# A state-space scan and a long convolution on one core: scanning pairs of time steps, and a written order for the instructions

## The chip, the cores and the metric

The kernel runs on one NeuronCore of one Trainium2 chip. The metric is the device time in microseconds of one execution. A core has TensorE (PE, matrix products into PSUM), VectorE (DVE), ScalarE (ACT), GpSimd (POOL) and SyncE (SP). Here SP, POOL and ACT also issue the DMA transfers, which sixteen DMA engines carry. Each engine works through its own instructions in the order in which the program gave them, and semaphores make one engine wait for another.

## The reference, cut to what matters

Two independent layers with L = 2048 times and D = 640 channels; their results stand side by side in the output.

```
# A: diagonal complex state space, 640 states
Lam_bar = exp(dt * Lam);  B_bar = ((Lam_bar - 1) / Lam)[:, None] * Bmat
h[t] = Lam_bar * h[t-1] + B_bar @ x[t]
a[t] = 2 * real(C @ h[t]) + Dskip * x[t]
# B: a shift of 4 taps on k, then a causal convolution over all 2048 times per channel
k_shift[t] = sum_j k[t-j] * shift_k[:, j]          # j = 0..3
kv = k_shift * v
y  = irfft(rfft(kv, 2L) * rfft(ssm_k, 2L))[:L]  + kv * ssm_D
b  = q * y
```

## The kernel before

**Layer A** goes by 4 chunks of 512 times (c) and 5 blocks of 128 states (j); n = 5c + j. `load_x` turns a chunk of x into `xT` on SP's queue. `pe_z` (L423) makes z = B x, 10 products of 512 columns for real and imaginary part; ACT moves z from PSUM to SBUF (L677). DVE rotates z by the phase of the state (`rotate`, L434 to L436, three steps of 1024 elements), which makes the recurrence real; it then scans with the real decay (`dve_scan`, L443, two scans of 512), and rotates back (`dve_out`). At the end of a chunk the last state is kept and turned by the phase of 512 steps (`dve_carry`). `pe_proj` (L466) multiplies h with C and (L472) adds D x through a diagonal matrix: for each of the 16 rows of 128 times 5 pieces, one per state block, each as soon as its h is there. ACT evicts (L476, `yo`), POOL stores (L480). Before that, C is multiplied by the complex factor of each state on PE (`pe_cs`, L349), with diagonal matrices that DVE builds (`dve_dg`, L335), and evicted by ACT (L353). B is turned on PE (L395).

**Layer B** goes by 5 groups G of 128 channels. `load_T` turns k and v on SP. The four taps are products of diagonal 128x128 matrices with shifted columns of kT (`pe_tap`, L509, 8 of 512 columns for each half of the times); DVE multiplies with v (L514). The convolution is a long transform in two steps: kv goes to DRAM and back so that rows of 128 times lie in the partitions (`store_kv`, `load_kv`); ssm_k is loaded in the same shape (`load_h`). The first step `pe_s1` (L525) has 16 products of 256 columns, the second `pe_s2` (L538 to L541) 64 of 128 columns, for kv and for ssm_k each; ACT evicts all of them (L529, L544). DVE multiplies the spectra (`dve_y`, L551 to L556). `pe_inv` (L565 to L568, 64 products) goes back, ACT evicts into `zz` (L572), SP turns zz into `Zt` (`turn_z`, L576), `pe_fin` (L586, 32 products) finishes, DVE multiplies with q (L591, `ob`), POOL stores (L596) and loads q (L580).

**The order.** `make_plan` lists the pieces of work with their engine, an assumed cost, what they depend on, and which piece takes or gives back one of the four double PSUM banks. `Plan.order` simulates the engines with those costs and a table of priorities (`PRIO`), and emits the pieces in the order that comes out. A name like `s2h3_1` is: second transform step of ssm_k for group 3, quarter 1; `s1k`, `s2k` the same for kv; `he`/`ke` endings are evictions; `tap`, `kv`, `kvo`, `kvs`, `y`, `inv`, `zs`, `zt`, `qi`, `fin`, `ob` follow the steps above; `p`, `yo`, `yd` are projection, eviction, store. SP's queue carries in order: x, k, v, C, h and the turns of zz; one entry that waits holds those behind it:

```
dma(f"zt{G}", "SP", 4.8, 3.7, [zs{G}_0..3] + [fin{G-1}_0, fin{G-1}_1], K.turn_z)
A(f"fin{G}_{hf}", "PE", 16 * P128, [f"zt{G}", "dRM"], ...)
A(f"ob{G}_{hf}", "DVE", PTT, [f"fin{G}_{hf}", f"qi{G}"], ...)
```

Of the kernel before, what the change touches and what calls it, by code (L numbers as in the profile page):

```python
# [22 lines left out]
NCH = L // CW  # L23
# [3 lines left out]
NH = 8  # L27
NPS = 4


class Plan:
# [5 lines left out]
    def add(self, name, eng, cost, deps=(), fn=None, lat=0.0, take=None, give=None, group=None):  # L37
        assert name not in self.items, name
        if eng == "PE":
            lat = max(lat, 0.2)  # L40
        self.items[name] = (eng, cost, [d for d in deps if d], fn, lat, take, give, group)

    def order(self, prio, hop=0.15):
        it = self.items
        succ = {n: [] for n in it}
        for n, x in it.items():
            for d in x[2]:
                succ[d.lstrip("~")].append(n)
        tail = {}
        todo = {n: len(succ[n]) for n in it}  # L50
        stack = [n for n in it if not todo[n]]
        while stack:
            n = stack.pop()
            x = it[n]
            tail[n] = x[1] + x[4] + max([tail[s] for s in succ[n]], default=0.0)
            for d in x[2]:
                d = d.lstrip("~")
                todo[d] -= 1
                if not todo[d]:
                    stack.append(d)  # L60
        assert len(tail) == len(it), [n for n in it if n not in tail][:5]
        rank = {n: -(tail[n] + prio.get(it[n][7], 0.0)) for n in it}
        need = {n: len(it[n][2]) for n in it}
        ready = {}
        for n in it:
            ready.setdefault(it[n][0], [])
            if not need[n]:
                ready[it[n][0]].append(n)
        free = dict.fromkeys(ready, 0.0)
        slots = [0.0] * NPS  # L70
        held, slot_of, done, start, seq = {}, {}, {}, {}, []
        while len(seq) < len(it):
            best = None
            for e, names in ready.items():
                c = []
                for n in names:
                    t = free[e]
                    for d in it[n][2]:
                        if d[0] == "~":
                            t = max(t, start[d[1:]] + it[d[1:]][1])  # L80
                        else:
                            t = max(t, done[d] + (hop if it[d][0] != e else 0.0))
                    if it[n][5] and it[n][5] not in held:
                        s = min(slots)
                        if s > 1e8:
                            continue
                        t = max(t, s)
                    c.append((t, rank[n], n))
                if c:
                    t0 = min(c)[0]  # L90
                    p, t, n = min((p, t, n) for t, p, n in c if t <= t0 + 0.05)
                    if best is None or (t, p) < best[:2]:
                        best = (t, p, n, e)
            t, _, n, e = best
            x = it[n]
            ready[e].remove(n)
            start[n], free[e], done[n] = t, t + x[1], t + x[1] + x[4]
            if x[5]:
                if x[5] not in held:
                    i = max((s, -i) for i, s in enumerate(slots) if s <= t + 1e-9)[1]  # L100
                    held[x[5]] = -i
                    slots[-i] = 1e9
                slot_of[n] = held[x[5]]
            if x[6]:
                slot_of[n] = held[x[6]]
                slots[held[x[6]]] = done[n] + hop
            seq.append((t, len(seq), n))
            for s in succ[n]:
                need[s] -= 1
                if not need[s]:  # L110
                    ready[it[s][0]].append(s)
        self.start, self.done = start, done
        return [n for _, _, n in sorted(seq)], slot_of


class Kernel:


    def __init__(self, ctx, tc, out, ins):
# [12 lines left out]
        t("ident", [128, 128])  # L132
        t("pidx", [128, 1], i32)
        t("c26", [128, 1], i32)
        for n in ("lre", "lim", "ldt", "dsk"):
            t(n + "_raw", [128, NT])
        for n in ("lre", "lim", "ldt", "dtf", "theta", "rho", "rr", "fr", "kf", "sin1", "aph1", "cos1", "nr", "ni", "den",
                  "t0", "rden", "g2re", "g2im", "ra"):
            t(n, [128, NT], f32)
# [4 lines left out]
        t("gb", [128, NT, 6])  # L144
        t("rots", [128, NT, 2], f32)
        t("rotc", [128, NT, 2], f32)
        for n in ("ca", "cb"):
            t(n, [128, NT, 2], f32)
        for i in range(2):
            t(f"last{i}", [128, NT, 2], f32)  # L150
            t(f"carry{i}", [128, NT, 2], f32)
        for n, k in (("r_hi", 1), ("r_lo", 1), ("bsh", 1), ("m_kk", 1), ("m_lo", 1), ("m_k1h", 1), ("m_ri", 1), ("m_k4", 2),
                     ("ccol", 8), ("r_ph", 32), ("r_q16", 32), ("m_ph", 32)):
            t(n, [128, k], i32)
        t("r_mask", [128, 8])
        t("m_mask", [128, 8])
        t("r_aph", [128, 32], f32)
        t("m_aph", [128, 32], f32)
        t("r_cv", [128, 32])
        t("m_cv", [128, 32], f32)  # L160
        t("sk_b", [128, NG, 4])
        t("dcol_b", [128, 16 * NG])
        t("lo", [128, CW], i32)
        t("aph", [128, CW], f32)
        t("R", [128, 32, 8])
        t("Mq", [128, 2, 16, 8])
        for n in ("Gre", "Gim", "nGim", "Hre", "Him", "nHim"):
            t(n, [128, 16, 128])
        t("tabs", [128, NT, 3, CW])
        t("BT", [128, 2, NT, D])  # L170
        t("Cs", [128, 2, NT, D])
        t("diagD", [128, NT, 128])
        for i in range(2):
            t(f"xT{i}", [128, NT, CW])
            t(f"Xs{i}", [128, 2, 1024])
            t(f"yo{i}", [128, D])
        for i in range(NZ):
            t(f"z{i}", [128, 2, CW])
        for i in range(NH):
            t(f"h{i}", [128, 2, CW])  # L180
        for n in ("rot_p", "rot_x", "w", "u"):
            t(n, [128, 2, CW])
        t("kT", [128, PAD + L])
        t("vT", [128, L])
        t("diagS", [128, 4, 128])
        for n in ("h_st", "kv_st", "qin", "ob"):
            t(n, [128, 16, 128])
# [3 lines left out]
        t("Y", [128, 2, L])  # L191
        t("pw_x", [128, 2, 1024])
        t("Zt", [128, 16, 2, 128])
        self.zz = self.pool.tile([128, 2 * NT * D], bf16, name="zz")
        self.Zs = self.zz[:, 0:4096].rearrange("p (i h k c) -> p i h k c", i=16, h=2, k=16)
        self.Bn = self.zz[:].rearrange("p (r j d) -> p r j d", r=2, j=NT)
        self.gph = self.Y[:].rearrange("p a n -> p (a n)").bitcast(i32).rearrange("p (q a b) -> p q a b", q=4, a=4)
        self.tph = self.qin[:].rearrange("p a c -> p (a c)").bitcast(i32).rearrange("p (q n) -> p q n", q=2)
        self.dg = self.ob[:].rearrange("p a c -> p (a c)")[:, 0:2 * 6 * 128].rearrange("p (b s n) -> p b s n", b=2, s=6)
# [16 lines left out]

    def pool_consts(self):
        g = self.nc.gpsimd
        g.iota(self.ident[:], pattern=[[1, 128]], base=0, channel_multiplier=-1, allow_small_or_imprecise_dtypes=True)
        g.iota(self.pidx[:], pattern=[[0, 1]], base=0, channel_multiplier=1)  # L220
        g.iota(self.c26[:], pattern=[[0, 1]], base=2 ** 26, channel_multiplier=0)
        g.iota(self.lo[:], pattern=[[1, CW]], base=0, channel_multiplier=0)

    def pool_consts2(self):
        g = self.nc.gpsimd
        g.iota(self.cmul[:], pattern=[[0, NT]], base=CW, channel_multiplier=0)
        g.iota(self.ccol[:], pattern=[[1, 8]], base=0, channel_multiplier=0)
        g.iota(self.r_ph[:].rearrange("p (k r) -> p k r", r=2), pattern=[[4, 16], [0, 2]], base=1, channel_multiplier=0)
        g.iota(self.r_q16[:].rearrange("p (k r) -> p k r", r=2), pattern=[[0, 16], [16, 2]], base=0, channel_multiplier=0)
        g.iota(self.m_k4[:], pattern=[[32, 2]], base=1, channel_multiplier=0)  # L230
        g.iota(self.m_ph[:].rearrange("p (h a) -> p h a", h=2), pattern=[[0, 2], [1, 16]], base=0, channel_multiplier=0)

    def dve_consts(self):
        v = self.nc.vector
        v.memset(self.hpi[:], PI / 2)
        v.memset(self.kT[:, 0:PAD], 0.0)
        s = v.tensor_single_scalar
        s(out=self.ident[:], in_=self.ident[:], scalar=0.0, op=ALU.is_equal)
        s(out=self.bsh[:], in_=self.pidx[:], scalar=19, op=ALU.logical_shift_left)

    def dve_consts2(self):
        s = self.nc.vector.tensor_single_scalar
        s(out=self.r_hi[:], in_=self.pidx[:], scalar=4, op=ALU.arith_shift_right)
        s(out=self.r_lo[:], in_=self.pidx[:], scalar=15, op=ALU.bitwise_and)
        s(out=self.m_kk[:], in_=self.pidx[:], scalar=3, op=ALU.arith_shift_right)
        s(out=self.m_lo[:], in_=self.pidx[:], scalar=7, op=ALU.bitwise_and)
# [296 lines left out]
    def act_s2(self, dst, o, ps):  # L543
        self.nc.scalar.copy(out=dst[:, :, o:o + 512], in_=ps[:])  # L544
# [278 lines left out]
```

## Time and profile before

| what | value |
|---|---|
| three runs | 270.46, 271.15, 277.94 us; median 271.15 |
| profiled execution | span 266.0 us from the first to the last instruction |
| around the span | 271.15 - 266.0 = 5.15 us, if the profiled execution took the median |
| PE / DVE / ACT / POOL busy | 216.5 / 213.0 / 160.1 / 47.5 us |
| mean granted TensorE clock | 0.958 |
| DMA | 34.02 MB, 128 GB/s over the span |

Busy time of PE counts products from their issue to their modelled end, and these overlap, so PE's rows are read by the distance of starts. The views used are the page, busy time by stretches, the chain of waits (the work that ended last, followed back), the groups kept apart by shape, and the DMA issues. A row of a group gives line, engine, operation, result and inputs, shape and count; then busy time and the mean ns of one; then the idle time of the engine before it and what ended it.

### The profile page before, as it was taken

The numbers are of one execution on the slowest core, as the hardware profiler recorded it, in microseconds if no ns is written. First come the engines' busy times: TensorE is split into PE (matmuls) and PEld (weight loads), VectorE is DVE, ScalarE is ACT, GpSimd is POOL, SyncE is SP. The second block draws the span as 40 slices with busy tenths as digits, with TensorE's granted clock in tenths as the row PEclk, the third lists the DMA queues.
The fourth block names the chain that finished last, engine by engine and source line by source line (L and its number), as shares of the span: only waits on it lengthen the run. The fifth ranks groups of instructions, "written<-read, shape, count | busy, mean of one in ns | idle before, by whom it ended". The sixth has DMA issues, their size and how long they took to land.

```text
span 266.0 us, 5042 instructions
## 1 busy us (share of the span) xinstructions
PE 216.5 (81%) x2106; PEld 157.9 (59%) x2106; DVE 213.0 (80%) x315; ACT 160.1 (60%) x201; POOL 47.5 (18%) x75
## 2 busy tenths in 40 slices
PE   0179748998998997999899989189997998199983
PEld 0035315564786665675688586187785977188762
DVE  2959996999999999999999999249958986079230
ACT  2828972978465867896837286129777886025112
POOL 8741307000021000000011024003002030013031
PEclk9999995999999999999999999959999999769998
DMA  4999936806994800092575299967951359608914
GB/s 98 239 211 212 173 79 163 153 2 120 167 218 124 204 0 2 0 188 53 120 191 138 76 185 215 151 158 153 162 85 79 83 97 152 93 27 170 196 51 128
DMA packets 81926, 34.02 MB, mean 128 GB/s; under 512 B 77552, under 2 KB 78832, under 8 KB 81904
## 3 DMA queue, kind: packets, MB, share of 16 engines
q1 hardware_dynamic: 75776, 19.27, 40.9%
q0 software_dynamic: 3760, 13.12, 22.4%
q10 hardware_dynamic: 2368, 1.31, 1.9%
q8 instruction: 16, 0.26, 0.4%
q14 instruction: 6, 0.05, 0.1%
HBM read 9.51 MB, written 7.86 MB: 65 GB/s over the span
## 4 chain that ended last, share of the span: by engine, by line
DVE 48%; DMA 27%; PE 13%; issue 7%; POOL 2%; ACT 1%; SPq 1%; POOLq 0%; DVEq 0%; ACTq 0%
DMA Zt<-zz 12%; DVE u L443 12%; DVE rot_p L434 7%; DVE rot_x L435 6%; DMA xT<-in_A_x_dram 5%; DMA out_dram<-yo 4%; DVE vT L514 4%; PE ps L423 4%; DVE w L436 3%; DMA kv_rows<-vT 3%; DVE h L436 3%; PE ps L586 3%; DMA h_st<-in_B_ssm_k_dram 2%; DVE pw_x L553 2%; DVE Y L551 2%
## 5 line engine op out<-in xcount | busy, mean ns | idle before, releaser
L423 PE MATMUL ps<-xT,BT 128*128 128x512 bf16 x200 | 47.5, 389 | 8.2 <-DMA xT<-in_A_x_dram 7.4
L466 PE MATMUL ps<-Cs,h 128*128 128x320 bf16 x320 | 52.0, 302 | 1.4 <-ACT yo L476 0.9
L423 PEld LDWEIGHTS <-BT 128*128 128x128 bf16 x200 | 19.6, 100 | 30.9 <-DVE t L326 7.7
L443 DVE TENSOR_TENSOR_SCAN u<-rr,carry,w 128x512 bf16<-128x512 f32 x30 | 36.9, 1272 | 0.5
L466 PEld LDWEIGHTS <-h 128*128 128x128 bf16 x320 | 29.4, 99 | 10.6 <-issue 1.8
L591 DVE TENSOR_TENSOR ob<-ps,qin 128x1024 bf16<-128x1024 f32 x10 | 12.0, 1221 | 25.2 <-PE ps L586 24.5
L572 ACT CAST zz<-ps 128x1024 bf16<-128x1024 f32 x20 | 19.3, 1024 | 19.4 <-PE ps L568 12.5
L677 ACT CAST z<-ps 128x1024 bf16<-128x1024 f32 x20 | 20.2, 1016 | 17.1 <-PE ps L423 14.4
L476 ACT CAST yo<-ps 128x640 bf16<-128x640 f32 x16 | 11.1, 697 | 29.1 <-PE ps L472 19.3
L544 ACT CAST Xs<-ps 128x1024 bf16<-128x1024 f32 x20 | 20.0, 1023 | 9.5 <-PE ps L541 8.6
L586 PE MATMUL ps<-Mq,Zt 128*128 128x128 bf16 x160 | 13.4, 257 | 13.9 <-DMA Zt<-zz 13.9
L529 ACT CAST As_kv<-ps 128x1024 bf16<-128x1024 f32 x20 | 19.4, 1054 | 5.5 <-PE ps L525 5.5
L544 ACT CAST Hf<-ps 128x1024 bf16<-128x1024 f32 x20 | 19.4, 1025 | 4.9 <-PE ps L541 3.3
L586 PEld LDWEIGHTS <-Zt 128*128 128x128 bf16 x160 | 12.3, 118 | 14.8 <-DMA Zt<-zz 14.5
L529 ACT CAST As_h<-ps 128x1024 bf16<-128x1024 f32 x20 | 19.4, 1035 | 2.6 <-PE ps L525 2.5
L517 POOL DMA_DIRECT2D kv_rows<-vT x5 | 2.8, 555 | 100.5 <-DVE vT L514 100.5
L509 PE MATMUL ps<-kT,diagS 128*128 128x512 bf16 x80 | 18.8, 380 | 1.1 <-ACT z L677 1.1
L565 PE MATMUL ps<-Y,Hre 128*128 128x128 bf16 x80 | 17.9, 224 | 1.8 <-DVE Y L555 1.8
L566 PE MATMUL ps<-Y,nHim 128*128 128x128 bf16 x80 | 17.9, 223 | 0.8 <-DVE Y L556 0.8
L538 PE MATMUL ps<-As_kv,Gre 128*128 128x128 bf16 x80 | 17.5, 219 | 1.0 <-DVE ob L591 0.7
L480 POOL DMA_DIRECT2D out_dram<-yo x16 | 8.8, 549 | 52.1 <-ACT yo L476 52.1
L568 PE MATMUL ps<-Y,Hre 128*128 128x128 bf16 x80 | 17.8, 223 | 0.0
(155 smaller groups left out, 581.1 us busy)
## 6 DMA issues: line engine op xcount, KB each, us to landing
h_st<-in_B_ssm_k_dram SPq DMA_DIRECT2D x5, 512.0 KB, 5.7
kv_rows<-vT POOLq DMA_DIRECT2D x5, 512.0 KB, 4.9
qin<-in_B_q_dram POOLq DMA_DIRECT2D x5, 512.0 KB, 9.4
kv_st<-kv_rows POOLq DMA_DIRECT2D x5, 512.0 KB, 6.7
out_dram<-yo POOLq DMA_DIRECT2D x16, 160.0 KB, 2.3
out_dram<-ob POOLq DMA_DIRECT2D x5, 512.0 KB, 5.5
zz<-in_A_B_re_dram ACTq DMA_DIRECT2D x1, 640.0 KB, 7.3
zz<-in_A_B_im_dram ACTq DMA_DIRECT2D x1, 640.0 KB, 10.0
```

The costliest lines, as they stand in the source:

```text
L423: self.nc.tensor.matmul(ps[:, r, :], lhsT=self.BT[:, r, k, j * 128:(j + 1) * 128], rhs=xT[:, k, :], start=(k == 0), stop=(k == NT - 1))
L434: tt(out=self.rot_p[:], in0=self.tabs[:, j, 0:1, :].to_broadcast([128, 2, CW]), in1=v, op=ALU.mult)
L443: self.nc.vector.tensor_tensor_scan(out=self.u[:, r, :], data0=rb, data1=self.w[:, r, :], initial=ini, op0=ALU.mult, op1=ALU.add)
L466: mm(ps[:, b, 0:320], lhsT=h[:, r, ts], rhs=self.Cs[:, r, j, c0:c0 + 320], start=(j == 0 and r == 0), stop=False)
L509: self.nc.tensor.matmul(ps[:, n, :], lhsT=self.diagS[:, j, :], rhs=self.kT[:, t0 - j:t0 - j + 512], start=(j == 0), stop=(j == 3))
L529: self.nc.scalar.copy(out=As[:, :, 32 * q:32 * q + 32].rearrange("p k (i c) -> p k i c", i=4), in_=ps[:].rearrange("p a n -> p (a n)").rea ...
L544: self.nc.scalar.copy(out=dst[:, :, o:o + 512], in_=ps[:])
L565: mm(o_re, lhsT=self.Hre[:, k1, :], rhs=yre, start=True, stop=False)
L566: mm(o_re, lhsT=self.nHim[:, k1, :], rhs=yim, start=False, stop=True)
L572: self.nc.scalar.copy(out=self.Zs[:, :, q // 2, k0:k0 + 8, :].rearrange("p i k c -> p k i c"), in_=ps[:].rearrange("p a n -> p (a n)").rea ...
L586: self.nc.tensor.matmul(psf[:, 128 * i:128 * i + 128], lhsT=self.Zt[:, 8 * hf + i, kh, :], rhs=self.Mq[:, kh].rearrange("p a c -> p (a c)" ...
L677: A(f"ze{n}", "ACT", EV, [f"z{n}"] + old, lambda ps, n=n: K.nc.scalar.copy(out=K.zt(n)[:], in_=ps[:]), give=f"z{n}", group=f"Z{n}")
```

## The change

1. **Scan over even times of pairs.** Two chunks of 512 pairs (1024 times) instead of four of 512 times. x is loaded as odd and even rows (`xT01`, `xT00`, ...: `load_x(c, p)`). For each block, `pe_zo` makes z of the odd rows, ACT puts it into `zo` (which keeps one column of history), and `pe_w` makes z of the even rows plus Lam times the odd z before it, with a diagonal matrix `diagL`. DVE rotates, scans with the squared decay and rotates back, for the even times alone; `dve_odd` rebuilds the odd ones from h of the even time and zo with scalar products and sums. So 10 blocks `rs`, `rout`, `od` instead of 20. The third step of a rotation is two halves of 512, since the sine table has lost its negated copy.
2. **First transform on row halves.** h and kv rows of 4 channels lie in partitions 0 to 63 and 4 more in 64 to 127 (`load_rows`, two transfers instead of one); `pe_s1` has 64-row products of 128 columns, two halves into two banks. The final matrix `Mq` and so `pe_fin` have 64 columns and a single product each, not two that are summed, and zz is turned in two halves (`zt{G}_0`, `zt{G}_1`).
3. **Taps on quadrants.** Diagonal 64x64 matrices; a copy `kS` of kT with its partition halves swapped (on POOL's queue, after kT has landed) feeds the quadrants that cross over.
4. **C scaled off PE.** ACT scales the real part by two factors, DVE adds the imaginary part in two steps of 640 for each block.
5. **Smaller ones.** Tables from two activations instead of four; nGim and nHim by a sign flip on DVE; one turn less (nHim); the spectra multiplied in place in Xs; q, its product and the phases share one tile `qb`, so that the q load of a group waits for the store of the group before; the projection is one piece for each 128 pairs and parity, after all five blocks; it is stored two rows of time at once.
6. **Order written out.** `Plan.order` and `PRIO` go; a list `ORDER` of 506 names with their PSUM bank gives the order.

```
-    def rotate(self, out, v, j, op):                            # tables: cos, sin, -sin
-        tt(out=out, in0=self.rot_p[:], in1=self.rot_x[:], op=op)
+    def rotate(self, out, v, j, back):                          # tables: cos, sin
+        for r in range(2):
+            tt(out=out[:, r, :], in0=self.rot_p[:, r, :], in1=self.rot_x[:, r, :], op=...)
...
+    def pe_w(self, n, rs, ps):
+        zo = self.zo(n, 1)                                      # odd z, one pair earlier
+        for r in rs:
+            self.pe_z(n, 0, r, o, False)                        # 5 products of 512
+            mm(o, lhsT=self.diagL[:, 0, j, :], rhs=zo[:, r, :], start=False, stop=False)
+            mm(o, lhsT=self.diagL[:, 2 - r, j, :], rhs=zo[:, 1 - r, :], start=False, stop=True)
...
+    def dve_odd(self, n):
+        v.tensor_scalar_mul(out=self.rot_p, in0=he, scalar1=self.lam[:, 0, j:j + 1])                     # 1024
+        v.tensor_scalar_mul(out=self.rot_x[:, 0, :], in0=he[:, 1, :], scalar1=self.lam[:, 2, j:j + 1])   # 512
+        v.tensor_scalar_mul(out=self.rot_x[:, 1, :], in0=he[:, 0, :], scalar1=self.lam[:, 1, j:j + 1])   # 512
+        v.tensor_tensor(out=self.rot_p, in0=self.rot_p, in1=self.zo(n, 2), op=ALU.add)
+        v.tensor_tensor(out=ho, in0=self.rot_p, in1=self.rot_x, op=ALU.add)
...
     def pe_tap(self, G, m, ps):
-        for n in range(2):
-            for j in range(4):
-                mm(ps[:, n, :], lhsT=self.diagS[:, j, :], rhs=self.kT[:, t0 - j:t0 - j + 512], ...)
+        for j in range(4):
+            for r in range(2):
+                rows = slice(64 * r, 64 * r + 64)
+                for v in range(2):
+                    cols = slice(64 * (r ^ v), 64 * (r ^ v) + 64)
+                    rhs = self.kS[rows, m, ...] if v else self.kT[rows, ...]
+                    mm(ps[cols, r, :], lhsT=self.diagS[rows, 4 * v + j, :], rhs=rhs, ...)
...
     def pe_s1(self, st, q, ps):
         for i in range(4):
-            mm(psf[:, 256 * i:256 * i + 256], lhsT=st[:, 4 * q + i, :], rhs=self.R, start=True, stop=True)
+            for h in range(2):
+                rows = slice(64 * h, 64 * h + 64)
+                mm(ps[:, h, :] (columns 4 * i of each 16), lhsT=st[rows, 4 * q + i, :], rhs=self.R[rows], ...)
...
+    def act_cs(self, j):                                        # for (r, s) in ((0, 0), (1, 1))
+        activation(out=self.ct[j % 2][:, r, 0:D], in_=self.Cs[:, 0, j, :], func=Copy, scale=self.gam[:, s, j:j + 1])
+    def dve_cs(self, j):
+        scalar_tensor_tensor(out=self.Cs[:, 0, j, :], in0=im, scalar=gam1, in1=self.ct[j % 2][:, 0, 0:D], mult, add)
+        scalar_tensor_tensor(out=im, in0=im, scalar=gam2, in1=self.ct[j % 2][:, 1, 0:D], mult, add)
...
     def pe_fin(self, hf, ps):
-        for i in range(8):
-            for kh in range(2):
-                mm(psf[:, 128 * i:128 * i + 128], lhsT=self.Zt[:, 8 * hf + i, kh, :], rhs=self.Mq[:, kh], ...)
+        for i in range(16):
+            mm(psf[:, 64 * i:64 * i + 64], lhsT=self.Zt[:, 16 * hf + i, :], rhs=self.Mq, start=True, stop=True)
```

The end of the written order, from the last scan block on (`@` gives the PSUM bank times two):

```
... rs7 s2h4_3@2 s2ke4_3@6 s2h4_1@0 s2he4_2@4 s2h4_0@6 s2he4_3@2 inv3_0@4 s2he4_1@0 inv3_1@2 rout7
s2he4_0@6 s2k4_2@0 zs3_1@2 s2k4_0@6 od7 zs3_0@4 s2k4_1@2 s2ke4_2@0 zt3_1 p1_0_0_0@4 s2ke4_1@2 y4_1 s2ke4_0@6 zt3_0
p1_0_1_0@6 yo1_0_0_0@4 y4_0 inv4_2@4 yo1_0_1_0@6 inv4_3@2 yd1_0 zs4_2@4 fin3_0@6 inv4_0@0 zs4_3@2 ob3_0@6
inv4_1@4 zs4_0@0 fin3_1@6 zs4_1@4 p1_2_1_0@2 ob3_1@6 zt4_0 od_3 p1_1_1_0@6 yo1_2_1_0@2 zt4_1 fin4_0@2 yo1_1_1_0@6
p1_2_0_0@4 qi4 p1_1_0_0@6 yo1_2_0_0@4 yd1_2 fin4_1@4 yo1_1_0_0@6 p1_3_0_0@0 yd1_1 ob4_1@4 ob4_0@2 p1_3_1_0@4 od_4
yo1_3_0_0@0 yo1_3_1_0@4 yd1_3
```

More of the change, by code (lines that the diff above doesn't have):

```diff
@@ L22 @@
 CW = 512
-NCH = L // CW
+NCH = 2
 NG = 5
@@ L26 @@
 NZ = 3
-NH = 8
+NH = 6
 NPS = 4
+SPLIT = set()
 class Plan:
@@ L35, in __init__, with add @@
         self.items = {}
-    def add(self, name, eng, cost, deps=(), fn=None, lat=0.0, take=None, give=None, group=None):
+    def add(self, name, eng, cost, deps=(), fn=None, lat=0.0, take=None, give=None, group=None, ring=0.0, nb=2):
         assert name not in self.items, name
[L39 to L113, printed above, removed]
@@ L116 @@
+        self.items[name] = (eng, cost, [d for d in deps if d], fn, lat, take, give, group, ring, nb)
 class Kernel:
@@ L475, in act_yo @@
-    def act_yo(self, c, i, ps):
-        self.nc.scalar.copy(out=self.__dict__[f"yo{i % 2}"][:].rearrange("p (b n) -> p b n", b=2), in_=ps[:, :, 0:320])
+            for j in range(NT):
+                h = self.ht(c * NT + j)
+                for r in range(2):
+                    mm(o[:, 0:320], lhsT=h[:, p, r, ts], rhs=self.Cs[:, r, j, c0:c0 + 320], start=(j == 0 and r == 0), stop=False)
+            pieces = [(d, max(c0, d * 128), min(c0 + 320, d * 128 + 128)) for d in range(NT)]
+            pieces = [q for q in pieces if q[1] < q[2]]
@@ L676, in make_plan @@
[L676 to L680 removed]
+            old = [f"rout{n - NZ}"] if n >= NZ else []
@@ L698, in make_plan @@
+            dma(f"yd{c}_{i}", "POOL", 0.55, 0.9, [f"yo{c}_{i}_{q}_{x}" for q in range(2) for x in range(np_)], lambda c=c, i=i: K.store_yo(c, i), group=f"P{c}")
     for G in range(NG):
@@ L740, in make_plan @@
[L740 to L745 removed]
+            A(f"y{G}_{hf}", "DVE", 6 * TT - 0.1, first, lambda hf=hf: K.dve_y(hf), group=k)
```

654 lines of the change are left out of this document (380 added, 274 removed), and 5 rows, old and new, of the table PRIO.

## The prediction

> **What bounds the kernel now.** I read the page's first lines, then busy time in five stretches, then the chain of waits, then the groups kept apart by shape, then the waits.
>
> ```profile
> span 266.0 us, 5042 instructions
> PE 216.5 (81%) x2106; PEld 157.9 (59%) x2106; DVE 213.0 (80%) x315; ACT 160.1 (60%) x201; POOL 47.5 (18%) x75
> 0.00:22.00 22.00, 7.74 (x60) 4.61 (x61) 13.75 (x43) 10.95 (x20) 13.85 (x29) 1.00 0.91 190
> 22.00:45.00 23.00, 16.89 (x73) 7.85 (x73) 20.65 (x35) 15.17 (x26) 6.58 (x14) 0.87 0.75 142
> 45.00:150.00 105.00, 98.75 (x931) 69.94 (x930) 102.67 (x148) 73.62 (x91) 8.29 (x12) 1.00 0.54 112
> 150.00:258.00 108.00, 89.72 (x1014) 73.05 (x1013) 75.80 (x91) 58.97 (x64) 16.54 (x19) 0.94 0.72 130
> 258.00:266.00 8.00, 3.44 (x34) 2.50 (x31) 0.08 (x1) 1.38 (x2) 2.26 (x3) 0.89 0.40 107
> ```
>
> The columns are PE, PEld, DVE, ACT, POOL, then clock, DMA share, GB/s. From 45 to 150 us DVE works 102.67 of 105: it is the bound. From 150 to 258 nobody is: DVE 75.80 of 108, at clock 0.94. What holds that stretch is the chain:
>
> ```profile
> 2.27 12.81 DMA xT<-in_A_x_dram
> 15.21 3.91 PE ps L423 x10
> 158.86 15.18 DMA Zt<-zz
> 174.08 3.60 PE ps L586 x32
> 181.00 1.31 PE ps L525 x12
> 182.31 2.16 PE ps L423 x10
> 214.69 16.95 DMA Zt<-zz
> L591 DVE TENSOR_TENSOR ob<-ps,qin 128x1024 bf16<-128x1024 f32 x10 | 12.0, 1221 | 25.2 <-PE ps L586 24.5 <-issue 0.6
> PE ps L586 <- DMA Zt<-zz: 13.9, 3, 6.9
> ```
>
> Twice the turn of zz into Zt takes over 15 us while PE and then DVE stand in their order before its use; in all PE waits 13.9 us for Zt and DVE 24.5 us for the products after it. At 174.08 a product then costs 3.60/32 = 112 ns.
>
> A PE row's duration overlaps its neighbours, so PE is counted by what products cost back to back:
>
> ```profile
> 67.14 2.34 PE L466 MATMUL ps<-Cs,h 128*128 128x320 bf16 x16
> 69.32 0.22 PE L538 MATMUL ps<-As_kv,Gre 128*128 128x128 bf16 x1
> 69.37 0.22 PE L539 MATMUL ps<-As_kv,nGim 128*128 128x128 bf16 x1
> 207.04 1.06 PE L586 MATMUL ps<-Mq,Zt 128*128 128x128 bf16 x16
> ```
>
> 512 columns: 2.16/10 = 216 ns. 320: (69.32-67.14)/16 = 136. 256: 1.31/12 = 109. 128: 56. Final ones: (1.06-0.22)/15 = 56. So PE has to stream: z 200x0.216 = 43.2; projection 320x0.136 = 43.5; D terms 4.5 (64 of 56 ns, 32 of about 30, an estimate by columns); first transforms 160x0.109 = 17.4; second 640x0.056 = 35.8; inverse 320x0.056 = 17.9; final 160x0.056 = 9.0; taps 80x0.216 = 17.3; C scaling 80x0.136 = 10.9; B turning 50x0.056 = 2.8. Sum 202 us of the 266. Both engines carry some 200 us; neither has much to give.
>
> **The change part by part.** DVE first; its rows:
>
> ```profile
> L443 DVE TENSOR_TENSOR_SCAN u<-rr,carry,w 128x512 bf16<-128x512 f32 x30 | 36.9, 1272 | 0.5
> L434 DVE TENSOR_TENSOR rot_p<-tabs,z 128x1024 bf16<-128x1024 bf16 x20 | 14.6, 729 | 0.1
> L435 DVE TENSOR_TENSOR rot_x<-tabs,z 128x1024 bf16<-128x1024 bf16 x20 | 13.7, 684 | 0.0
> L436 DVE TENSOR_TENSOR w<-rot_p,rot_x 128x1024 bf16<-128x1024 bf16 x20 | 13.8, 692 | 0.7
> L553 DVE TENSOR_TENSOR pw_x<-Xs,Hf 128x2048 bf16<-128x2048 bf16 x10 | 12.2, 1218 | 0.0
> L335 DVE TENSOR_TENSOR ob<-ident,gb 128x768 bf16<-128x768 bf16 x5 | 4.7, 953 | 2.1 <-PE ps L349 2.1
> L340 DVE TENSOR_TENSOR diagD<-ident,dsk_raw 128x640 bf16<-128x640 bf16 x1 | 0.8, 815 | 0.0
> L238 DVE TENSOR_SCALAR ident<-ident 128x128 bf16<-128x128 bf16 x1 | 0.2, 195 | 0.2 <-POOL ident L219 0.2
> ```
>
> *Scan of pairs.* A block of 512 times costs 2x(729+684+692) + 2x1272 = 6.75 us, 20 of them 135. After, ten blocks of 512 pairs. The third step of each rotation is now two halves: 1024 elements cost 692 and 2048 cost 1218, so a half is about 692-263 = 429 and the pair 166 ns dearer. That makes 6.75+0.33 = 7.08 for the even times. The odd times: one scalar product of 1024, two of 512, two sums of 692. No row shows a scalar product of that size; below it is the 195 ns of 128 elements, above it the 692 (429) of a two-tensor step as large. I take the middle, 443 and 312 each: 2.45 us. Ten blocks: 95 us, 40 less than now (bounds 45 and 35). The steps of Y, kv and ob keep their sizes and counts, and ACT's z evictions theirs.
>
> *C scaled off PE.* Ten two-source steps of 640 on DVE, at the 815 row: +8.2; five steps of 953 go: -4.8; PE loses its 10.9; ACT swaps ten evictions for ten scalings:
>
> ```profile
> L353 ACT ACTIVATE Cs<-ps 128x640 bf16<-128x640 f32 x10 | 6.5, 701 | 7.3 <-PE ps L349 7.3
> L373 ACT ACTIVATE tabs<-qin 128x512 bf16<-128x512 int32 x5 | 3.1, 630 | 0.0
> L368 POOL TENSOR_TENSOR qin<-lo,Fi 128x512 int32<-128x512 int32 x5 | 5.2, 1040 | 11.4 <-ACT aph L207 9.8 <-DVE Fi L300 1.6
> ```
>
> I keep 701 for them (nothing), with 815 (+1) above. Two activations per table instead of four, one fewer per G block: -9x0.63 and -5x0.63, ACT about 151. POOL does five phase steps more, 5.2 us; it was busy 13.85+6.58 of the first 45 us, so they go into its idle time (the first table would be 1 us later without it).
>
> *Once.* diagL, 1920 elements, from 815 for 640 and 953 for 768: +2.2. Two sign flips of 2048, between 195 and 1218, taken 0.7 each (one H turn on SP goes for it): +1.4. DVE in all: 213-40+8.2-4.8+2.2+1.4-1 for smaller constants = 179.
>
> *PE.* diagL adds 40x0.216 = +8.6. Taps: 160 products of 64x64 weights and 512 columns instead of 80. If four run side by side, 40x0.216 = 8.6; if none, 34.6. No row has such a product; I take 12, near the first, since the four quarters share neither rows nor result. First transforms: 320 products of 64 rows and 128 columns instead of 160 of 256: 9.0 if halves run in pairs, 17.9 if not; I take 13.5, the middle. Final products halve their columns; each still loads 128x128 weights, so between 4.6 and 9.0, taken 9.0. PE in all: 202+8.6-10.9-5.3-3.9 = 191.
>
> The Trainium skill, "TensorEngine Tiling (Array Packing)", section Tiling Modes, says that going from one tiling mode to another drains the engine. The written order changes mode 49 times. A drained 128-column product costs its 219 ns (L541 row below) in place of 56, so by the page 49x0.163 = 8 us come on top, by my sum none; no run shown so far has a change of mode.
>
> *Where it lies.* **Start:** x now comes as two turned loads, odd rows first. The first product still starts at 15.2; 3.91 (half clock) + 2.16 + 14x0.216 + 1.0 of eviction let DVE begin at 25.3, not 22. The second x turn pushes kT, vT, C and h on SP back by at most its 8.8 us:
>
> ```profile
> xT<-in_A_x_dram SPq DMA_TRANSPOSE x4, 8.8
> 260.69 1.52 ACT L476 CAST yo<-ps 128x640 bf16<-128x640 f32 x2 [5.56 <-PE ps L472]
> ```
>
> That is hidden by the z products that PE now has first (5x2.16 + 5x3.0 = 26 us), and costs up to 8.8 if they run out.
> **PE path:** 15.2 + (191-2.8) + 4.5 after the last product (the last yo begins at 260.69+1.52-0.69 = 261.5 of 266.0) = 207.9.
> **DVE path:** by 22 us it had done 13.75; diagL and two diagonals of 0.8 join that, so at 25.3 179-17 = 162 are left, and it could end at 187. But all products of the second half of x, eight of 20x0.136+0.28 = 3.0 us, need the last block, od7, and after it DVE has only two Y halves (2x1.22+2x0.69 each) and four ob left, 12 us: od7 ends at 175 or later, then PE has 24 + 3.6 + 3.6 us left and 4.5 follow: 211. Both paths end within 3 us of each other, so neither covers the other's waits.
> **New waits:** the taps wait for kS, a POOL copy behind kT; on POOL the kv rows of the group before queue behind it (kvs0 behind kS1). The nearest row is the kv store (first below), 4.9 us to landing. Between one group's taps and the next one's the order has 10 us and more of PE's other work: nothing, and 4.9 a group if that cover is gone. q and the result share a tile, so a q load waits for the store before it:
>
> ```profile
> kv_rows<-vT POOLq DMA_DIRECT2D x5, 512.0 KB, 4.9
> qin<-in_B_q_dram POOLq DMA_DIRECT2D x5, 512.0 KB, 9.4
> out_dram<-ob POOLq DMA_DIRECT2D x5, 512.0 KB, 5.5
> DMA to landing us min/median/max: 8.4/11.9/17.0
> L541 PE MATMUL ps<-As_h,Gre 128*128 128x128 bf16 x80 | 17.6, 219 | 0.0
> ```
>
> At the end ob3 to ob4 takes 1.2+0.5+5.5+9.4 = 16.6, then 2.4+0.5+5.5 = 8.4: 25.0 after fin3. PE over the same stretch has four halves of the projection and two final groups, 13.8, two more halves, 6.0, and the 4.5: 24.3. So +0.7, counted as 1.
> **Zt** (fourth row) is turned in halves and the order puts 7 to 12 us of other products between the last inverse and the final products. That is about a whole turn's 8.4 to 11.9, so part of the wait stays. I take the 13.9 us that PE waits for Zt now as the allowance for all waits (bounds: 2, the idle time of DVE from 45 to 150, and 32, all its idle time from 150 to 258).
> **Sum:** the later path, 207.9 to 211, taken 209, + 14 + 1 = a span of 224. The profiled execution's span is 266.0, the median of the runs 271.15, so 5 us lie around it: **229 us**.
>
> **Rivals.** (a) *Tiles do not run side by side:* the change of taps and first transforms then doesn't do what it says. Taps 34.6 and transforms 17.9 are 27 more: 256. For it: no row shows two products at once. Against: quarters share no rows.
> (b) *The array empties at each change of mode:* 49 times 219-56 ns, 8 more: 237. For it: a lone product lasts 219 ns; against it: nothing in the trace. The Trainium skill's page "TensorEngine Tiling (Array Packing)" has this rule under Tiling Modes.
> (c) *The stall only moves:* the 32 us stay, 18 more than allowed: 247. For it: fixed orders with four banks, one of which zo9 holds for some 20 us. Against: Zt halves, no late x load before Zt on SP.
> (d) *Hardly a wait is left:* 2 instead of 14, 217, as DVE ran from 45 to 150. Against: there PE had slack, and now it has none.
> (e) *Slower:* narrow products are not overlapped at all. At 219 ns each the 320 transforms cost 70, and the 160 taps at 380 cost 61:
>
> ```profile
> L509 PE MATMUL ps<-kT,diagS 128*128 128x512 bf16 x80 | 18.8, 380 | 1.1 <-ACT z L677 1.1
> L525 PE MATMUL ps<-R,h_st 128*128 128x256 bf16 x80 | 10.9, 273 | 3.8 <-DVE vT L514 2.2 <-DVE h_st L498 0.8 <-ACT yo L476 0.7
> ```
>
> That is 105 us more on PE's path, 334. It decides from 42 us on, 88 ns more for each of the 480 than counted. Against: today's products overlap (56 of 219).
>
> **How the numbers follow.** Chances: forecast 0.52 (own range 219 to 238), (a) 0.12, (b) 0.13, (c) 0.10, (d) 0.08, (e) 0.05. The range runs from 214 (the paths with no wait but the last) to 256 (all of (a)); outside are half of (a), some of (c), (e) and a little of (d), under 0.2. Two per cent, 5.4 us, is about what a measurement of this kernel can tell from no change. All cases but (e) stay under 265.7; of (c) 0.02 goes further, and 0.01 of (e) ends short of 276.6: faster 0.93, same 0.03, slower 0.04.
>
> **What would show it.** Right: DVE busy near 179 and PE's L465 and L381 rows as now; sixteen tap products in about 1.2 us; DVE's first rotation near 25; PE waiting on Zt in single microseconds; both engines busy through 30 to 200. Wrong: sixteen taps in 3.5 us (a); gaps of 0.16 us around each L544 run (b); ob waits of 5 us and more for every group (c); a scalar product of 1024 at 692 or more, which would put 5 us on DVE.

## The result and the profile after

The changed kernel takes **247.07 us** (median of 4 runs, 246.06 to 248.01); the kernel before took 270.8 beside it. The ratio is 0.917, 95% interval 0.909 to 0.925: 24 us faster, where 42 were forecast. The time lies in the range of 214 to 256, but outside the likeliest case's own 219 to 238. Some executions take over 1.5% longer than the fastest of the same kernel, most of them at a lower clock; where undisturbed times are given they leave these out, and the profiles of e1, e2, e3, e6, e8 and e11 come from such executions.

The profiled execution took 247.58 us, its span is 245.7. Two lines of its page, and busy time in eight stretches, cut where DVE starts its rotations, stands still, or ends the last block of the scan (columns: us, PE, PEld, DVE, ACT, POOL, clock, DMA share, GB/s):

```profile
span 245.7 us, 5441 instructions
PE 197.2 (80%) x2295; PEld 140.8 (57%) x2306; DVE 180.7 (74%) x303; ACT 152.0 (62%) x187; POOL 64.8 (26%) x91
...
0.00:30.80 30.80, 16.29 (x89) 9.20 (x91) 16.29 (x60) 15.88 (x28) 24.27 (x45) 0.94 1.11 140
30.80:121.10 90.30, 78.41 (x825) 50.56 (x830) 88.98 (x143) 62.12 (x78) 19.80 (x23) 0.98 0.92 160
121.10:131.20 10.10, 3.63 (x40) 2.48 (x43) 0.01 (x1) 2.30 (x3) 3.49 (x4) 0.66 0.74 132
131.20:149.80 18.60, 18.50 (x268) 13.48 (x263) 17.07 (x20) 14.50 (x16) 3.46 (x5) 1.00 1.03 198
149.80:180.60 30.80, 27.02 (x421) 22.25 (x420) 18.98 (x29) 24.45 (x27) 5.26 (x6) 1.00 0.73 128
180.60:208.40 27.80, 25.35 (x354) 20.99 (x352) 27.15 (x41) 23.20 (x25) 2.32 (x2) 0.94 0.42 87
```

DVE's work is what was forecast, 180.7 against 179. From 30.8 to 121.1 it hardly stops (88.98 of 90.30). The loss lies in two places: it begins late, at 30.8, and between 121 and 181 it does 36 us of work in 59.5. The waits name what it waits for (engine and line, whom for, us in total, times, longest):

```profile
POOL qb L598 <- DMA out_dram<-qb: 26.9, 4, 10.0
ACT yo L477 <- DMA out_dram<-yo: 10.8, 2, 7.2
DVE vT L532 <- PE ps L527: 10.1, 1, 10.1
PE ps L558 <- ACT yo L477: 6.6, 1, 6.6
PE ps L603 <- DMA zz<-zz: 6.2, 5, 2.7
DVE qb L608 <- DMA qb<-in_B_q_dram: 5.2, 1, 5.2
DVE qb L608 <- ACT Hf L564: 4.8, 1, 4.8
```

PE's wait for Zt, 13.9 before, is 6.2 (now the tile is named zz). New are a wait of ACT for a store of the A rows (yo), which holds PE and through it DVE for 10.1 us, and a wait for q. The chain of waits shows the first of them from its root (start, us, what):

```profile
113.56 1.22 POOL kS L501 x2
114.77 11.97 DMA out_dram<-yo
126.82 0.70 ACT yo L477
127.57 0.27 PE ps L558
...
129.43 2.52 PE ps L527 x16
...
137.34 0.55 PE ps L544 x16
...
218.23 0.47 PE ps L603 x16
```

On POOL's queue the two kS copies are issued right ahead of a yo store of 320 KB. That store takes 11.97 us to land (3.4 is the median of the eight). ACT, whose next eviction goes into the same yo tile, stands until then; PE finds no free bank, DVE no taps. The copies themselves, which the same taps read, land just as late, about 126.6:

```profile
L501 POOL DMA_DIRECT2D kS<-kT x2: 612/617/622, 113.6 to 114.2; - x2
DMA to landing us min/median/max: 12.3/12.4/12.4
```

So with the copies landing then, these taps could not have run much earlier even with a free yo tile; in the chain the one wait hides the other. The transfers as a whole, after (first two lines) and before (last two), queue, packets, MB, share of 16 engines' span:

```profile
q1 hardware_dynamic: 73936, 18.75, 52.6%
q0 software_dynamic: 4368, 14.46, 26.3%
```
```profile
q1 hardware_dynamic: 75776, 19.27, 40.9%
q0 software_dynamic: 3760, 13.12, 22.4%
```

Nearly the same bytes on q1, yet a packet takes 0.526x245.7x16/73936 = 28 ns where it took 0.409x266.0x16/75776 = 23. With both queues the 16 DMA engines are busy 79% of the span against 63%: 194 us of 245.7. That is a third sum as large as PE's and DVE's, and the prediction did not make it. It is not a sum of work like theirs, though: about the same packets took longer here, and the share reads above 1 in some stretches (1.11 in the first row above).

### The profile page after: what moved, and what is told of

It reads as the page before. It is cut to its first block, busy times and chain, and to the rows that moved or that the text cites. A ratio compares the mean times of both kernels' runs of the same rounds, so it can differ in the third digit from the quotient of the medians.

```text
span 245.7 us, 5441 instructions
## 1 busy us (share of the span) xinstructions
PE 197.2 (80%) x2295; PEld 140.8 (57%) x2306; DVE 180.7 (74%) x303; ACT 152.0 (62%) x187; POOL 64.8 (26%) x91
## 3 DMA queue, kind: packets, MB, share of 16 engines
q1 hardware_dynamic: 73936, 18.75, 52.6%
## 4 chain that ended last, share of the span: by engine, by line
DVE 15%; issue 13%; PE 12%; DMA 12%; POOL 2%; ACT 1%; DVEq 1%; POOLq 0%; ACTq 0%
DMA out_dram<-yo 5%; DMA zz<-zz 4%; DMA qb<-in_B_q_dram 3%; PE ps L465 2%; DVE rot L571 2%; DVE Xs L572 2%; PE ps L381 2%; DVE Xs L574 2%; PE ps L527 2%; DVE z L430 2%; DVE vT L532 1%; POOL out_dram L613 1%; DVE rot L419 1%; DVE rot L420 1%; DVE qb L608 1%
## 5 line engine op out<-in xcount | busy, mean ns | idle before, releaser
L608 DVE TENSOR_TENSOR qb<-ps,qb 128x1024 bf16<-128x1024 f32 x10 | 12.1, 1219 | 26.0 <-PE ps L603 16.0
L558 PE MATMUL ps<-As_kv,Gre 128*128 128x128 bf16 x80 | 18.5, 231 | 8.8 <-ACT yo L477 6.6
L559 PEld LDWEIGHTS <-nGim 128*128 128x128 bf16 x160 | 16.5, 103 | 12.4 <-issue 10.7
L559 PE MATMUL ps<-As_h,nGim 128*128 128x128 bf16 x80 | 18.3, 229 | 1.3 <-DVE nGim L343 1.3
L532 DVE TENSOR_TENSOR vT<-ps,vT 128x1024 bf16<-128x1024 f32 x10 | 11.9, 1213 | 10.1 <-PE ps L527 10.1
L558 PE MATMUL ps<-As_h,Gre 128*128 128x128 bf16 x80 | 18.3, 229 | 1.3 <-DVE qb L608 1.0
L582 PE MATMUL ps<-Xs,Hre 128*128 128x128 bf16 x80 | 17.6, 219 | 1.4 <-DVE Xs L574 1.4
L561 PE MATMUL ps<-As_kv,Gre 128*128 128x128 bf16 x80 | 18.5, 232 | 0.0
L560 PE MATMUL ps<-As_kv,Gim 128*128 128x128 bf16 x80 | 18.5, 232 | 0.0
L559 PE MATMUL ps<-As_kv,nGim 128*128 128x128 bf16 x80 | 18.5, 232 | 0.0
L560 PE MATMUL ps<-As_h,Gim 128*128 128x128 bf16 x80 | 18.3, 228 | 0.0
L561 PE MATMUL ps<-As_h,Gre 128*128 128x128 bf16 x80 | 18.3, 228 | 0.0
```

The source lines that it names most:

```text
L532: self.nc.vector.tensor_tensor(out=self.vT[:, ts], in0=ps[:].rearrange("p a n -> p (a n)"), in1=self.vT[:, ts], op=ALU.mult)
L558: mm(o_re, lhsT=self.Gre[:, k1, :], rhs=re, start=True, stop=False)
L559: mm(o_re, lhsT=self.nGim[:, k1, :], rhs=im, start=False, stop=True)
L560: mm(o_im, lhsT=self.Gim[:, k1, :], rhs=re, start=True, stop=False)
L561: mm(o_im, lhsT=self.Gre[:, k1, :], rhs=im, start=False, stop=True)
L582: mm(o_re, lhsT=self.Hre[:, k1, :], rhs=yre, start=True, stop=False)
```

## The experiments

**e1, e2, e3: take the two waits away.** If they are waits for shared tiles, other tiles end them.

```diff
e1:  yo tile of row block i, first half of x:  i % 2  ->  (0, 1, 1, 0)[i]
e2:  q of groups 2 and 4 in xT01 and xT00 (used up by then); ORDER: qi2 moved up behind yo0_3_1_0,
     qi3 and qi4 behind yd0_3 (they stood behind od_2 and od_3)
e3:  both
```

> Edit: in the first half of x, row block 2 takes the yo tile of block 1 and block 3 that of block 0 (the changed kernel: 2 after 0, 3 after 1). Block 1's store is issued at 110.1 us, block 0's at 114.8 behind the result store of 512 KB, and landed at 126.7. Theory A (shared tiles hold the engines): ACT's wait of 7.2 us for the yo store, PE's 6.6 behind it and DVE's 10.1 before the taps' product go; the time falls by 7 to 10 us, to 237 to 240. Theory B (the stall only moves: transfers are too slow, whichever is waited for): DVE's idle time from 120 to 180 us stays near 22 us and the time is within 2 us of 247.

> Edit: q of groups 2 and 4 is loaded into xT01 and xT00 (the first half of x, used up by then), and the loads of q are issued as soon as their tile is free, not behind the store of the group before. Theory A: DVE's wait of 5.2 us for q at 180.6 goes, and nothing else changes before it: 4 to 6 us less, 241 to 243. The tail stays, since the last two products wait for PE (14.7 us), not for q. Theory B: the q load of group 2 was only one of several late things there (the turned zz2 comes at the same time), DVE waits for PE's product in its place: within 2 us of 247.

> Both edits. Theory A: the two waits lie one after the other on DVE's path, so both gains add: 11 to 16 us less, 231 to 236, with od7's end near 193 to 196 in place of 208.4 and the 37 us after it unchanged. Theory B: less than 4 us from both together.

Measured: e1 248.66 us median, its one undisturbed run 243.17; e2 254.43 (251.05 and 251.27 undisturbed); e3 254.67 (251.1 and 253.51). No 11 to 16 us came. By their undisturbed runs e2 and e3 are 4 to 6 us above the changed kernel, though the ratios to the kernel before beside them, 0.924 and 0.929, have intervals that overlap its 0.917; for e1 a single run of 243.17 leaves a small gain open. The first theory falls. In e1 DVE's wait for the taps' product fell from 10.1 to 2.95 us. What the taps waited for was now the copy kS, and a longer wait came up 20 us later:

```profile
121.63 0.37 PE L530 MATMUL ps<-kS,diagS 64*64 64x512 bf16 x1 [0.88 <-DMA kS<-kT]
...
144.85 0.69 DVE L419 TENSOR_TENSOR rot<-tabs,z 128x1024 bf16<-128x1024 bf16 x1 [11.34 <-ACT z L399]
...
PE ps L547 <- DMA kv_st<-kv_rows: 7.1, 1, 7.1
```

Now the q load, the kv rows, a yo store and a kv store all start on POOL between 121.8 and 126.2, and SP's turned load of kT at 123.6 beside them. kT lands after 14.8 us, where the corresponding one took 7.5, and the kv rows after 12.7, where they took 7.1. It is the kv rows that PE waits for (last row, of the waits), and through PE's order z and DVE. In e2 the turns of zz of group 2 run beside the q loads and a result store; from the view of their line, first the changed kernel, then e2:

```profile
L595 SPq DMA_TRANSPOSE zz<-zz x2: 2907/3854/4801, 166.5 to 171.4; - x2
DMA to landing us min/median/max: 7.1/7.9/8.8
```
```profile
L595 SPq DMA_TRANSPOSE zz<-zz x2: 5530/5686/5843, 167.0 to 172.5; - x2
DMA to landing us min/median/max: 11.7/15.8/19.9
```

In the changed kernel one q load, of group 2, is issued at 172.79 beside the second turn. In e2 the loads of groups 3 and 4 are issued there, at 173.77 and 174.93; in the changed kernel these two go out at 192.76 and 227.64. DVE's wait of 5.2 us for q is gone, and it waits 4.32 and 8.25 us for the two products of the turned halves.

**e4, e7: an earlier start.** In the changed kernel x00 was issued at 10.9 and landed at 24.8, beside the load of the rest of B.

```diff
- dma("B1", "ACT", ..., ["~l_lre"], ...)
+ dma("B1", "SP",  ..., ["~x00"],  ...)
e4:  ORDER: zo0, z0 ahead of bt6 bt5 bt3 bt4 bt2; lam, dL ahead of them on DVE
e7:  e4, and bte2, bte3 by ACT instead of DVE, bt2 and bt3 first
```

> Edit: the large B load (1.28 MB, before on ACT's queue from the start) is issued on SP behind both x turns; on PE the first block's two products go ahead of the rest of B's turning. x01 was issued at 2.3 us and landed at 16.8, x00 at 10.9 and landed at 24.8. Theory A (the B load crowds the x turns, and x00's landing sets the first rotation): x00 lands near 15, DVE's first rotation starts at 22 to 25 instead of 30.8, DVE's path is 4 to 6 us shorter and so is the kernel, unless the rest of B is now late for the second block. Theory B (a turned load of x takes its 14 us by itself): x00 lands at 24 to 25 as before, B comes later still, and the kernel is 3 to 8 us slower.

> Edit: e4's order, and the turned B of the other blocks is evicted by ACT instead of DVE, what the second block needs first. In e4 DVE's first rotation came at 19.6 us (30.8 in the changed kernel), but its evictions stood behind the first scan, PE waited 4.7 us for them and the second block came at 39.9. Theory A: the second block follows by 31, 5 to 8 us of the 11 last, and the kernel ends 5 to 8 us earlier: 239 to 242. Theory B': the kernel is held by the transfers of 100 to 150 us, in e4 the taps' product came at 131.5 as in the changed kernel (131.2) despite the earlier start; then 245 to 249 again.

Measured: e4 247.45 (245.85 to 249.82); e7 246.66 (undisturbed 244.69, 245.15 and 248.17). The turned load landed in half the time (view of its line, the changed kernel for both loads, then e4 for the first):

```profile
L373 SPq DMA_TRANSPOSE xT<-in_A_x_dram x2: 4997/6764/8532, 2.3 to 10.9; - x2
...
DMA to landing us min/median/max: 13.9/14.2/14.5
```
```profile
L373 SPq DMA_TRANSPOSE xT<-in_A_x_dram x1: 4246/4246/4246, 2.3 to 2.3; - x1
...
DMA to landing us min/median/max: 7.3/7.3/7.3
```

So the B load did crowd x, and DVE's first rotation came at 19.60 in e4 and 23.14 in e7, not 30.80. The kernel gained nothing in e4 and at most some 2 us in e7: the second block and DVE's other work did not follow as early (e4's DVE worked 22.06 of the 30 us from 30 to 60; the changed kernel 28.86), and the taps' product that DVE waits for came at 131.49 and 126.89 against 131.21.

**e5, e6, e8: the changed kernel again, POOL's order, and all together.** e5 has no edit; it stands on the same chip as e6 to e11.

```diff
e6:  e1's yo tiles; ORDER: qi1 behind kvo3 (was ahead of kvs2); q of groups 2 and 4
     in xT01 and xT00, qi2 to qi4 at their old places
e8:  e6 and e7 together
```

> The changed kernel as it is, beside the next three on one chip. All theories: 245 to 249, DVE idle 10 us before the taps' product at 131, 5 us before the result product at 180.6.

> Edit: the yo tiles swapped as in e1; q of group 1 is issued on POOL behind the kv store of group 3, not ahead of the kv rows of group 2; q of groups 2 and 4 gets xT01 and xT00, each at its old place in the queue. In e1 the yo wait was gone, but behind the q load, which sat 7.4 us on POOL for the store of the result before it, the kv rows, a yo store, a kv store and SP's kT load all started within 5 us, kT took 15 us to land and DVE lost 11.3 us there. Theory A' (POOL's queue, held by the q load, bunches the transfers): kv rows of group 2 start near 115 and not 123 to 127, kT lands in 8 us or less, the idle time of DVE from 120 to 150 falls from 12 us to under 5, and that before the product at 180 goes: 8 to 15 us less than the changed kernel, 232 to 239. Theory B' (the transfers of 100 to 150 us need all their time, in whatever order, with the DMA share at 1.0): the idle time only changes its place, time within 2 us of 247.

> e6 and e7 together. Theory A and A': gains add, 226 to 234. Theory B': 245 to 249, or less only by what e6 gives.

Measured: e5 246.68 (244.97 to 248.62); e6 255.78 (one undisturbed run, 249.48); e8 256.99 (undisturbed 255.64 to 257.27). e6 moved the bunch from 122 to 165 us: od_1's store and q of group 2 went out together at 164.55 and 165.71, the turns of zz issued at 166.2 and 171.5 took 17.8 and 14.8 us, and DVE waited 10.42 us for the product at 185. That theory falls too: as in e1 and e2, the transfer that started earlier ran beside another, which then landed later. e8 shows the same: its DVE waits 10.90 us for the product at 190.

**e9, e10: fewer transfers instead of earlier ones.**

```diff
e9:   swap_k(): no copies;  rhs = kS[...] if v else kT[...]  ->  rhs = kT[...]
e10:  swap_k(): no copies;  diagS [128, 8, 64] -> [128, 4, 128] over ident
      16 products of 64x64 weights per call -> 8 of 128x128, kT alone
```

> The copies of k with swapped halves (kS, ten of 129 KB on POOL's queue) are left out; the tap products that read kS read kT in its place, so half the taps' sum is of other rows; all engine work is as in the changed kernel. Theory C (the 16 DMA engines are the third full resource: 0.82 of 245.7 us busy, 1.0 from 0 to 60 and from 90 to 150): with 1.3 MB of 35 and one link of the chain kT, kS, taps gone, the turned kT and vT land sooner and the kernel ends 4 to 8 us earlier, 239 to 243. Theory P (PE's and DVE's streams with the written order set the time): DVE's 10 us before the taps' product at 131 come from the yo tile and stay, under 2 us of difference.

> The quadrant part of the change undone, the rest kept: 80 tap products with 128x128 diagonals and kT alone, no kS copies. PE gets 80x0.216 = 17.3 us of taps in place of ten times 1.3 to 1.4, about 13.5: 4 us more; no change of tiling mode there; DVE's diagonal stays at 0.69. Theory C: as e9 less what PE's 4 us cost, 239 to 245, so the quadrants bring nothing here. Theory P: 2 to 4 us slower, 248 to 251.

Measured: e9 240.76 (239.47 to 241.60), ratio to before 0.903 (0.887 to 0.919); e10 242.84 (240.57 and 240.92 undisturbed), ratio 0.904 (0.879 to 0.929). Beside e5 on the same chip e9 is 6 us faster, and no run of the one reaches a run of the other (up to 241.60, from 244.97); e10 is 6 us faster by its two undisturbed runs, 4 by the medians. The ratios to the kernel before are less sharp: their intervals overlap that of the changed kernel. e9 leaves out the swapped rows that half of the tap products need and serves the time alone; e10 computes what the reference asks. The chain at the place shown above, e5, then e9, then e10:

```profile
115.20 1.22 POOL kS L501 x2
116.41 10.38 DMA out_dram<-yo
126.87 0.70 ACT yo L477
```
```profile
112.78 8.63 DMA out_dram<-yo
121.49 0.70 ACT yo L477
...
123.28 1.85 PE ps L523 x32
```
```profile
112.74 6.78 DMA out_dram<-yo
119.59 0.70 ACT yo L477
```

In e9 ACT goes on 5.4 us earlier, in e10 7.3. For e9 the steps up to the taps' product can be told apart. The eviction that fills the yo tile comes 2.95 us earlier (111.79, not 114.74); the store follows it 0.7 us more closely, without the copies ahead of it on POOL; it lands 1.75 us sooner; and PE's products from there to the taps' product take 1.7 us less, since they run 0.06 us apart and not 0.11 (the clock granted from 126.87 to 131.44 in e5 is 0.50, from 121.49 to 124.38 in e9 1.00). Together 7.1 us: DVE gets the product at 124.38, not 131.44. From there to the end of the span it is 115.4 us in both, and 114.5 to 116.9 in the profiles of the changed kernel, e4, e7, e10 and e12. So in these seven profiles the time is decided by when this product comes, and what is won up to it is kept. In e1 it is not: the product comes at 122.92, and 124 us follow.

What theory C said of kT and vT is borne out in part: vT's median landing, 9.6 us in the changed kernel and 8.9 in e5, is 8.2 in e9 and 8.3 in e10, but kT's, 7.5 in both, is 8.4 and 7.3. The copies' place in POOL's queue is worth 0.7 us; how the rest divides between the traffic that they add and the taps' waiting for them, no run separates. By e10 nothing clear of the scatter is lost when PE gets its 128x128 tap products back: the quadrants of the change saved PE time at the price of transfers, and here the price was the larger.

**e11, e12: the pieces put together.**

```diff
e11:  e7 and e1's yo tiles; q of group 2 in xT01, issued when that is free;
      q of group 4 in xT00, issued right behind qi3
e12:  e10 and e7
```

> e7's start and e1's yo tiles; q of group 2 goes to xT01 as soon as that is free (160 us), that of group 4 to xT00 right behind the load of group 3's, ahead of the last turns of zz. In e2 and e6 the loads of q ran beside the turns of zz of group 2, which then took 12 to 20 us to land (7.1 and 8.8 in the changed kernel), and DVE lost 10 us there. Theory C (a load beside a turn stretches the turn): with the loads in stretches in which nothing is turned the turns stay at 6 to 9 us, the wait of 5 us before the product at 180 goes, 236 to 242. If it is the tile xT and not the time of the load that costs, 250 or more as in e2 and e6.

> e10 (full taps, no kS) and e7 (B behind x on SP, evictions by ACT) together. Theory C (transfers hold the stretch from 90 to 150 us; with the kS copies gone there is room, so an earlier start is no longer swallowed whole): DVE's first rotation at 23, the taps' product near 119 in place of 123.2, the end 3 to 5 us before e10's: 236 to 239. Theory B' (the stall moves again): 240 to 244, as e10.

Measured: e11 249.27 (undisturbed 244.42 and 247.72), as the changed kernel; e12 242.47 (undisturbed 240.67 to 243.72), ratio to before 0.901 (0.890 to 0.913), as e10. In e11 the turns of zz of group 2 landed after 10.3 and 7.4 us, not the 11.7 to 19.9 of e2: with the q load moved away they come back towards the changed kernel's 7.1 and 8.8. e11 lost its DVE waits for q but has new ones, for the taps' product at 151.04 (5.66 us) and z at 140.80 (4.92). e12 rotates from 21.48 and stands at the taps' product at 122.62, e10 rotates from 30.13 and stands there at 123.21. So the earlier start is swallowed again, and before this product: the taps' product ahead of it comes at 105.09 and 105.48. The best version found is the changed kernel with the full taps, 240.6 to 240.9 undisturbed; the earlier start on top of it gained nothing beyond the scatter, and other tiles and loads were not tried on top of it.

## Why the prediction was right and wrong

**DVE, right.** 179 were forecast, 180.7 came. The two unknowns, by shape (busy, mean ns):

```profile
L443 DVE TENSOR_SCALAR rot<-h,lam 128x1024 bf16<-128x1024 bf16 x10 | 4.8, 484 | 0.1
L444 DVE TENSOR_SCALAR rot<-h,lam 128x512 bf16<-128x512 bf16 x10 | 3.5, 348 | 0.0
L445 DVE TENSOR_SCALAR rot<-h,lam 128x512 bf16<-128x512 bf16 x10 | 4.1, 411 | 0.0
L303 DVE SCALAR_TENSOR_TENSOR Cs<-Cs,gam,As_kv 128x640 bf16<-128x640 bf16 x3 | 2.6, 879 | 0.0
```

484, 348 and 411 for 443 and 312; 879 for 815. Together 2.4 us more than taken, the first three inside their bounds. ACT came out at 152.0 for 151. DVE's 32 us less (213.0 to 180.7) are the largest saving; that the 24 us come from them is argued, since no run has the new scan alone.

**PE, right in direction, taken too dear.** Tap products: 32 in 1.85 us (e9's row), so four run in 0.23 us, hardly more than one of 128x128 (0.216), side by side: rival (a) is refuted, and 160 cost 9.3, not 12. First transforms: 16 in 0.55, 11.0 for all, not 13.5. Final products of 64 columns: 16 in 0.47, 4.7, not 9.0; their length goes with the columns although each loads 128x128 weights. PE's stream is so about 9 us shorter than the 191 forecast. That this gave nothing is argued from e10: its full taps take PE 80x0.216-9.3 = 8 us more, and its undisturbed runs are no slower than e9's.

**Rival (b), the mechanism seen, its price not.** Around one run of first transforms in the timeline (start, us):

```profile
143.53 0.22 PE L585 MATMUL ps<-Xs,Hre 128*128 128x128 bf16 x1
143.68 0.62 PE L544 MATMUL ps<-R,kv_st 64*128 64x128 bf16 x16
144.23 0.23 PE L582 MATMUL ps<-Xs,Hre 128*128 128x128 bf16 x1
```

The next product starts 0.15 us after the last full one, where full ones follow at 0.055; leaving costs as much, if the 16 run in pairs at 0.056 (0.55 less 0.45). A change of mode thus costs about 0.1 us, 49 of them 5 us by estimate, and not 0.163 and 8; the sum had none. (The 16 in 0.55 above already hold their way out.) The Trainium skill ("TensorEngine Tiling (Array Packing)", Tiling Modes) has the rule that a change of mode drains the engine; the 0.1 us of these rows agrees with it. e10 has fewer such changes, but the chain above puts its gain elsewhere.

**The start, a wrong step.** "The first product still starts at 15.2", and DVE at 25.3. It was 18.26, and 30.80:

```profile
18.26 4.48 PE L381 MATMUL ps<-xT,BT 128*128 128x512 bf16 x19
...
24.84 2.23 PE L381 MATMUL ps<-xT,BT 128*128 128x512 bf16 x5 [2.09 <-ACT zz L144]
...
30.80 0.69 DVE L419 TENSOR_TENSOR rot<-tabs,z 128x1024 bf16<-128x1024 bf16 x1 [4.19 <-ACT z L399]
```

The second x turn was counted as pushing back only what is queued behind it. But z0 needs it itself, and starts at 24.84, when it lands; the engine named in the brackets had long been done. That is 5.5 us of DVE's path, but not of the time: e4 and e7 began earlier still and gained 0 to 2 us.

**The waits, the step that failed.** The prediction took 15 us for all waits and named Zt's 13.9 as their measure. Zt's did fall, to 6.2. Between 30.8 and 208.4, however, DVE works 88.98+0.01+17.07+18.98+27.15 = 152.2 of 177.6 us: 25.4 us of waits. The kS copies were "nothing, and 4.9 a group if that cover is gone". In the taps at 131 they took 12.4 us to land and not 4.9, which PE's other work did not cover, and the yo store that ACT needed was slow beside them. Without them the kernel is 6 us faster (e9). The q load behind the store in one tile was counted as 1 us at the end; it shows as 5.2 us at 180.6, though e2 and e6, which took it out of there, came out slower.

**The sum.** In spans, 224 forecast and 245.7 measured: start 5.5, waits 25.4 for 15 is 10.4, DVE 152.2 for 150 before od7 is 2, the stretch after od7 37.3 for 36 is 1, and the DVE path of 211 should have been taken, not 209. Together 21 of 21.7. Against that stand some 3 us in the time around the span: 5 were taken from a span and a median of different executions, 247.58-245.7 = 1.9 is what one execution shows. Rival (c), the stall only moves, fits the mechanism best, but its sign "ob waits of 5 us and more for every group" came in part: 5.2 and 14.7 us (the last for PE), one of 4.8, two groups with little. That its 247 is the measured time is luck: it kept 32 us of waits and the old start, and the runs show 25.4 and a start 5.5 us later. And the range held the time thanks to an upper end that belonged to (a), which is refuted.

**What stays open.** Of the 18 us between forecast and result, 6 are the kS copies, shown by e9 and, less sharply, by e10. The rest is shown as place (start, ob at 150 and at 180), not as a cause that an edit removes: e2, e4, e6, e7, e8, e11 and e12 each moved one of these waits, and time was lost at another. No run shortened the 115 us behind the taps' product. The transfers are the likely reason, with a DMA share near 1.0 up to 60 us and around 90 to 150, but no run here lightened them beyond kS. Whether another written order of the same transfers could give the 12 us was not found out.

## What to carry to other kernels

Sum the transfers like an engine: the share of the DMA queues times the span, before and after, beside PE's and DVE's sums; an edit that trades engine time for a copy can lose by it, as the quadrants did here. A wait for a transfer was not removed here by another tile or an earlier issue (e1, e2, e6): ask which turn or store the freed transfer will then run beside, and which in-order queue it stands in. When variants differ, look for the point from which the rest takes the same time in all of them; what counts lies ahead of it. And a split load has to be checked for what needs its second half, not only for what is queued behind it.

## What the runs showed of the hardware

The same transfer took very different times to land in different company: 320 KB of yo 3.4 us at the median and 12.0 behind two copies and a 512 KB store; half of zz, turned, 7.1 to 8.8 us in the changed kernel and 11.7 to 19.9 in e2, with more q loads beside it; x, turned, 7.3 us, and 14.5 beside the load of B. Products that PE ran at a granted clock of 0.50 (e5, after the wait for the yo store) stood 0.11 us apart, at 1.00 (e9) 0.06. The Trainium skill ("DMA: Bandwidth & Descriptors", Issuing engines are not separate DMA queues) says that transfers of all issuing engines run on the same 16 DMA engines and interleave; these rows agree. Four 64x64 tap products of 512 columns ran in 0.23 us, hardly more than one of 128x128 takes (0.216).
